# An attention and two mixture layers in one kernel: another order of the first loads, and the expert embeddings normalized in another stage

## The chip, the cores and the metric

The kernel runs on one core of one Trainium2 chip. The metric is the device time of one execution in microseconds (us). The kernel before takes 813.03 us, the median of three runs.

## The reference

Three layers follow each other, all in float32.

```python
attn = softmax(mask(q @ k.T / 8)) @ v          # 4 batches, 8 heads, 576 tokens, 64 wide
x = attn as [2304, 512]                        # heads side by side
x = ((x @ w_a) * (x @ w_b)) @ w_out            # w_a, w_b: 512 x 1536; w_out: 1536 x 512
en = expert_emb / (norm(expert_emb) + 1e-6)    # 8 x 512
logits = (x / (norm(x) + 1e-6)) @ en.T / tau   # the best of 8 experts for each token
out = gate * (relu(x @ w1[e]) @ w2[e])
```

The mask keeps a window of 32 keys in four heads, and every fourth of 128 keys in the other four. `w_a`, `w_b` and `w_out` are float64 in memory, so they come as 64-bit words ("doubles"), which the kernel turns into float32 itself.

## The kernel before, in words

The order of all instructions is written out by hand (`tc.manual_schedule()`, L1027): each engine, and each DMA queue, works through its own instructions in program order. SyncE (SP) issues nearly all loads and stores, one queue in program order; an issue that waits for a buffer holds all issues behind it.

**Precision.** Every large matrix product is made of three products of high and low parts (`mm3`, L582: high by high, high by low, low by high). `split` (L545) makes the parts: ScalarE (ACT) copies the high part (L546), VectorE (DVE) or GpSimd (POOL) subtracts it for the low part (L547).

**Doubles.** `conv_load(i)` (L495) loads block i of 18 (twelve of the a/b weights, 0 to 11, six of the output weights, 12 to 17; 1 MB each) into one of two `c64` buffers, or into the buffer of `wo` for blocks 2, 5, 8, 11. `conv_steps(i)` (L513) converts it in four steps: one on ACT (L526) and three on DVE (L528, L530, L532). `conv_store` (L508) stores the result for the later batches.

**First attention** (loop at L1047, blocks i = 0 to 12). In block i the scores of row block i are made (mask and `sc` on TensorE, PE, L410 and L416; `amx` on DVE, L426; `least` on POOL), the exponentials of block i-1 (ACT, L439), the transposes of block i-3 (L452) and the product with `v` of block i-4 (L468), whose result is split into `x0h` (ACT, L483) and `x0l` (DVE, L485). Between them stand one warm-up matmul (`keep_warm`, L762), steps of the conversion of doubles 0 and 1 as `CONV_STEPS` says, four quarter splits of `ab` 0 as `SPLIT0` says (`ab_split_part`, L549), and the first a/b products in blocks 10 and 11. The scores of block i use the banks of block i-2, so they wait for its exponentials. `qkt` and `vt` each have two buffers and come in thirds of a batch, three blocks each.

**Steps f = 0 to 11 of a batch** (`f_step`, L605). Each makes one 128-wide column block of x @ w_a and x @ w_b in four PSUM banks (`mm`), multiplies them (`g`, L619), and carries one block of the next batch's attention along. At f the split of `ab` f+1 is made; in batch 0 the doubles of block f+2 are converted, and block f+5 is loaded (L636). In batch 0 the exponentials of the attention follow the split on ACT.

**x1(b)** (`x1_run`, L707) makes the output projection of batch b in twelve steps; each needs a split of `wo`, made one step ahead (`x1_weights`, L680). In x1(0) the conversion of doubles 14 to 17 goes along, two steps for each block: the ACT step stands ahead of the split in even steps.

**Embeddings.** `setup` (f=2) loads them into `esb`, a tile of the `cv` pool beside the `c64` buffers. `setup2` (L140) normalizes them on DVE with a Newton iteration (`inv_norm`, L114), in the middle of f=6 of batch 0. `setup_en` (L148), in f=10, stores them to memory, transposes them on PE and copies them. `open_rows` (L753) closes `cv` in step 10 of x1(0) and opens the pool of `rows` and `en_a` in its place. At the start of batch 1 `en_a` and `en_b` are loaded (L1107), then `xs` is prefilled over the first four steps (L169), two issues ahead of each `ab_load` (L540).

The constants that the change touches stand at L50 to L57.

Of the kernel before, what the change touches and what calls it, by code (L numbers as in the profile page):

```python
# [48 lines left out]
N_WARM = 1  # L49
CONV_STEPS = (0, 0, 0, 0, 1, 1, 1, 1, 0, 1, 1, 1, 1)  # L50
CONV1 = 3
SPLIT0 = (8, 8, 9, 9)
PRE = (10, 11)
TEVAC_DVE = 5
ORDER = (0, 1, 1, 2, 3, 2)
LAG = 3
WARM_TO = 10  # L57
REBIAS = 2.0 ** -112
# [22 lines left out]
def fused_kernel(ctx: ExitStack, tc: tile.TileContext, qk, v, wab, wout, w1, w2, emb, tau, cst, msk, out, dbg=None):  # L81
# [31 lines left out]

    def inv_norm(ss, p, n, extra=None):  # L114
        x = ss
        yi = rt.tile([128, 8], I32, tag="nyi", name="nyi")[:p, :n]
        y = rt.tile([128, 8], F32, tag="ny", name="ny")[:p, :n]
        t = rt.tile([128, 8], F32, tag="nt", name="nt")[:p, :n]
        nc.vector.tensor_scalar(out=yi, in0=x.bitcast(I32), scalar1=1, scalar2=None, op0=ALU.logical_shift_right)
        nc.vector.tensor_scalar(out=y.bitcast(I32), in0=yi, scalar1=-1.0, scalar2=float(0x5F3759DF), op0=ALU.mult, op1=ALU.add)  # L120
        for _ in range(3):
            nc.vector.tensor_tensor(out=t, in0=y, in1=x, op=ALU.mult)
            nc.vector.tensor_tensor(out=t, in0=t, in1=y, op=ALU.mult)
            nc.vector.tensor_scalar(out=t, in0=t, scalar1=-0.5, scalar2=1.5, op0=ALU.mult, op1=ALU.add)
            nc.vector.tensor_tensor(out=y, in0=y, in1=t, op=ALU.mult)
        nc.vector.tensor_tensor(out=t, in0=y, in1=x, op=ALU.mult)
        nc.vector.tensor_scalar(out=t, in0=t, scalar1=1e-6, scalar2=None, op0=ALU.add)
        if extra is not None:
            nc.vector.tensor_tensor(out=t, in0=t, in1=extra, op=ALU.mult)
        nc.vector.reciprocal(out=y, in_=t)  # L130
        return y

# [7 lines left out]
    def setup2(e_sb, t_sb):  # L140
        junk = rt.tile([128, DM], BF16, tag="jl", name="ejunk", bufs=1)[:E, :]
        ss = rt.tile([E, 1], F32, tag="ess", name="ess", bufs=1)
        nc.vector.scalar_tensor_tensor(out=junk, in0=e_sb, scalar=1.0, in1=e_sb, op0=ALU.mult, op1=ALU.mult, accum_out=ss)
        rinv = inv_norm(ss, E, 1, extra=t_sb)
        nc.vector.tensor_scalar(out=e_sb, in0=e_sb, scalar1=rinv, scalar2=None, op0=ALU.mult)
        return e_sb

    def setup_en(junk):  # L148
        nc.sync.dma_start(out=en_d, in_=junk)
        tp = ps.tile([128, 4, E], F32, tag="rps", name="etp")  # L150
# [344 lines left out]
    def conv_load(i):  # L495
        if i < len(conv_src):
            if i < NF and i % 3 == 2:
                c64[i] = mp.tile([128, 2048], I32, tag="wo", name="c64w", bufs=1)
            else:
                c64[i] = cv.tile([128, 2048], I32, tag="c64", name="c64")  # L500
# [44 lines left out]
    def split(raw, hi, lo, eng=None):  # L545
        nc.scalar.activation(out=hi, in_=raw, func=AF.Copy)  # L546
        (eng or nc.vector).tensor_tensor(out=lo, in0=raw, in1=hi.bitcast(F32), op=ALU.subtract)  # L547

    def ab_split_part(n, q):  # L549
        if q == 0:  # L550
            ab_hl[n] = (ap.tile([128, 1024], F32R, tag="abh", name="abh"), ap.tile([128, 1024], F32R, tag="abl", name="abl"))
        w = slice(256 * q, 256 * q + 256)
# [4 lines left out]
    def ab_split(n):  # L557
        if n < n_ab:
            hl = (ap.tile([128, 1024], F32R, tag="abh", name="abh"), ap.tile([128, 1024], F32R, tag="abl", name="abl"))
            split(ab_raw.pop(n), *hl)  # L560
# [44 lines left out]
    def f_step(b, f, at_cur, at_mid, at_prev, extra, extra2):  # L605
# [27 lines left out]
        if f < NF - 2:  # L633
            ab_load(n + 2)
        if b == 0 and n != 9:
            conv_load(n + 5 if n < 9 else n + 4)  # L636
        cg = iter(())
# [42 lines left out]
    def x1_weights(b, i, n_i):  # L680
# [3 lines left out]
        if b == 0:  # L684
            conv_store()
            if i % 2 == 0:
                x1_conv[:] = [conv_steps(NF + 2 + i // 2)]
# [7 lines left out]
        if b == 0:  # L695
            conv(x1_conv[0], 1)
            if i % 2:
                conv_load(NF + 4 + i // 2)
        if not last:
# [6 lines left out]

    def x1_run(b, rows_at, hook):  # L707

# [3 lines left out]
        for i in range(NF):  # L712
            x1_weights(b, i, NF)
            if i == 0:
                g_lows()
            if i == rows_at:
                open_rows()
            hook(i)
# [308 lines left out]
    with tc.manual_schedule():  # L1027
# [19 lines left out]
        for i in range(NJ + LAG + 1):  # L1047
            if i in (3, 6, 9):
                load_qk()
            if i == CONV1:  # L1050
                conv_load(1)
                nc.sync.dma_start(out=c_sb, in_=cst)
            if i in (5, 9):
                load_v()
            if i == 6:
# [8 lines left out]
            if LAG + 1 <= i:  # L1064
                gr[i - LAG - 1].av()
            keep_warm(N_WARM if i < WARM_TO else 0, "mm1" if (i + 1 - LAG) % 2 else "tp")
            if 1 <= i < NJ + 1:
# [18 lines left out]
        for b in range(B):  # L1086
# [9 lines left out]
            for f in range(NF):  # L1096
# [15 lines left out]
                if b == 0 and f == 2:  # L1112
                    es.append(setup())
                if b == 0 and f == 6:
                    extra2.append(lambda: es.append(setup2(*es[0])))
                if b == 0 and f == 10:
                    extra2.append(lambda: setup_en(es[1]))
                if b == 1 and f < 4:
# [8 lines left out]
            if not last:  # L1127
                x1_run(b, 10 if b == 0 else None, lambda i: [next(steps, None) for _ in range(2)])
                for _ in steps:
# [228 lines left out]
```

## Time and profile before

| | |
|---|---|
| runs | 812.54, 813.03, 814.74 us (median 813.03) |
| profiled execution | 813.63 us, span 811.80 us |
| PE busy | 789.0 us, 97% |
| weight loads of PE busy | 729.0 us, 90% |
| DVE busy | 519.7 us, 64% |
| ACT busy | 410.5 us, 51% |
| POOL busy | 217.4 us, 27% |
| mean granted clock of TensorE | 0.987 of full speed |
| moved by DMA | 136.18 MB, mean 168 GB/s |

The span is what the profiler sees of one execution; the time of that execution has some 1.8 us around it. A row of a timeline has a start and a duration in us, the engine, the line of the kernel, the operation, output and inputs, and how often it stands there in a row; in square brackets is the idle time of its engine just before it and what ended it. Matmuls overlap, so they start closer together than their durations say. A granted clock of 1.00 is 2.4 GHz, one of 0.50 is 1.2 GHz.

### The profile page before, as it was taken

How to read it: one execution, taken by the hardware profiler on the slowest of the kernel's cores; microseconds unless marked ns; L12 is line 12 of the kernel's file. 1: busy time of each engine (PE TensorE's matmuls, PEld its weight loads, DVE VectorE, ACT ScalarE, POOL GpSimd, SP SyncE). 2: the span in 40 equal slices, each digit the busy share in tenths (PEclk: the TensorE clock that was granted, in tenths of full speed). 3: DMA queues.
4: the chain of work that ended last, by engine and by line, in shares of the span. 5: the costliest groups of instructions: out<-in, count | busy, mean ns of one | idle time of the engine just before them, and what ended most of it. 6: DMA issues, size and time to landing. Idle time of an engine off the chain costs nothing.

```text
span 811.8 us, 15994 instructions
## 1 busy us (share of the span) xinstructions
PE 789.0 (97%) x6112; PEld 729.0 (90%) x6112; DVE 519.7 (64%) x1153; ACT 410.5 (51%) x1014; POOL 217.4 (27%) x274
## 2 busy tenths in 40 slices
PE   7999998999999999999999999999999999999995
PEld 4799887789999889999989999999898999999994
DVE  4788888738876426787745884455666565666670
ACT  5666565345654225565324443454564544755651
POOL 3343244016353303544221334331110001111111
PEclk9899999999999999999999999999999999999998
DMA  9886676799433322241153222635565636655720
GB/s 288 297 253 205 222 217 230 251 322 342 156 105 108 125 78 80 94 134 61 51 165 117 92 78 91 222 130 197 183 208 191 203 125 194 209 166 183 234 77 26
DMA packets 40295, 136.18 MB, mean 168 GB/s; under 512 B 4084, under 2 KB 4340, under 8 KB 37777
## 3 DMA queue, kind: packets, MB, share of 16 engines
q1 hardware_dynamic: 37120, 125.54, 47.4%
q0 software_dynamic: 3088, 9.52, 3.1%
q8 instruction: 50, 0.82, 0.4%
q14 instruction: 37, 0.30, 0.1%
HBM read 109.67 MB, written 25.80 MB: 167 GB/s over the span
## 4 chain that ended last, share of the span: by engine, by line
PE 77%; issue 6%; DVE 6%; DMA 5%; ACT 5%; POOL 0%; POOLq 0%; DVEq 0%; SPq 0%
PE mm L584 11%; PE mm L586 10%; PE mm L585 10%; PE xr L585 4%; PE xr L586 4%; PE xr L584 4%; PE hp L585 3%; PE hp L586 3%; PE hp L584 3%; PE ytp L586 2%; PE ytp L585 2%; PE ytp L584 2%; DMA out_dram<-yo,ixi 2%; PE av L468 2%; PE sc L416 2%
## 5 line engine op out<-in xcount | busy, mean ns | idle before, releaser
L584 PE MATMUL mm<-x0h,abh 128*128 128x288 f32 x768 | 235.0, 306 | 1.5 <-DVE g L619 1.5
L586 PE MATMUL mm<-x0h,abl 128*128 128x288 f32 x768 | 226.8, 295 | 0.0
L585 PE MATMUL mm<-x0l,abh 128*128 128x288 f32 x768 | 226.7, 295 | 0.0
L584 PEld LDWEIGHTS mm<-x0h,abh 128*128 128x128 f32 x768 | 144.6, 188 | 6.7 <-DVE g L619 1.6
L585 PEld LDWEIGHTS mm<-x0l,abh 128*128 128x128 f32 x768 | 144.8, 188 | 0.0
L586 PEld LDWEIGHTS mm<-x0h,abl 128*128 128x128 f32 x768 | 144.6, 188 | 0.0
L623 POOL TENSOR_TENSOR gl<-g,gh 128x288 fp32r<-128x288 f32 x96 | 94.6, 991 | 114.7 <-ACT gh L622 114.6
L547 DVE TENSOR_TENSOR wl<-raw,wh 128x1024 fp32r<-128x1024 f32 x60 | 73.0, 1222 | 53.1 <-ACT wh L546 52.9
L547 DVE TENSOR_TENSOR wo<-wor,wo 128x512 fp32r<-128x512 f32 x60 | 46.4, 774 | 66.2 <-ACT wo L546 61.6
L982 POOL DMA_INDIRECT out_dram<-yo,ixi x23 | 27.3, 1188 | 204.6 <-ACT yo L981 157.9
L619 DVE TENSOR_TENSOR g<-a,mm 128x288 f32<-128x288 f32 x96 | 43.3, 451 | 54.9 <-PE mm L586 47.2
L546 ACT ACTIVATE wo<-wor 128x512 fp32r<-128x512 f32 x60 | 37.8, 630 | 78.6 <-PE xr L586 54.3
L622 ACT ACTIVATE gh<-g 128x288 fp32r<-128x288 f32 x96 | 42.4, 442 | 66.2 <-DVE g L619 66.2
L584 PE MATMUL hp<-xTh,wh 128*128 128x352 f32 (+6 forms) x224 | 68.9, 308 | 0.0
L546 ACT ACTIVATE abh<-abr 128x1024 fp32r<-128x1024 f32 (+1 forms) x51 | 51.1, 1007 | 33.2 <-DVE abr L532 20.8
L585 PE MATMUL hp<-xTl,wh 128*128 128x352 f32 (+6 forms) x224 | 67.7, 302 | 0.0
L586 PE MATMUL hp<-xTh,wl 128*128 128x352 f32 (+6 forms) x224 | 67.6, 302 | 0.0
L547 DVE TENSOR_TENSOR abl<-abr,abh 128x1024 fp32r<-128x1024 f32 x47 | 57.4, 1221 | 15.8 <-ACT abh L546 15.0
L546 ACT ACTIVATE wh<-raw 128x1024 fp32r<-128x1024 f32 x64 | 67.0, 1053 | 0.0
L434 POOL TENSOR_SCALAR least<-amx 128x4 f32<-128x4 f32 x36 | 23.5, 652 | 152.3 <-DVE amx L431 100.2
L584 PE MATMUL xr<-wo,gh 128*128 128x512 f32 x156 | 61.8, 396 | 2.4 <-ACT wo L546 2.1
L585 PE MATMUL xr<-wo,gh 128*128 128x512 f32 x156 | 61.8, 396 | 0.6 <-DVE wo L547 0.6
(218 smaller groups left out, 1715.6 us busy)
## 6 DMA issues: line engine op xcount, KB each, us to landing
raw<-in_w_dram SPq DMA_DIRECT2D x64, 512.0 KB, 4.2
abr<-wab SPq DMA_DIRECT2D x36, 512.0 KB, 3.4
wor<-wout SPq DMA_DIRECT2D x24, 512.0 KB, 3.4
qkt<-in_qk_dram SPq DMA_DIRECT2D x12, 832.0 KB, 8.4
c<-in_wab_dram SPq DMA_DIRECT2D x8, 1024.0 KB, 12.7
vt<-in_v_dram SPq DMA_DIRECT2D x12, 576.0 KB, 4.6
xs<-rows SPq DMA_DIRECT2D x8, 781.5 KB, 16.6
wab<-abr SPq DMA_DIRECT2D x12, 512.0 KB, 5.0
```

What stands on the lines that cost most here:

```text
L416: nc.tensor.matmul(out=self.sc[odd][64 * q:64 * q + 64, h, :], lhsT=t[64 * p:64 * p + 64, pr, 64 * jj:64 * jj + 64], rhs=t[64 * p:64 * p + ...
L434: nc.gpsimd.tensor_scalar(out=self.least, in0=mx, scalar1=0.125, scalar2=None, op0=ALU.mult)
L468: nc.tensor.matmul(out=self.o[64 * p:64 * p + 64, pr, :], lhsT=t[:, jj, 64 * h:64 * h + 64], rhs=self.aT[:, pr, 64 * (p ^ pr % 2):64 * (p ...
L546: nc.scalar.activation(out=hi, in_=raw, func=AF.Copy)
L547: (eng or nc.vector).tensor_tensor(out=lo, in0=raw, in1=hi.bitcast(F32), op=ALU.subtract)
L584: nc.tensor.matmul(out=out_, lhsT=lh, rhs=rh, start=first, stop=False)
L585: nc.tensor.matmul(out=out_, lhsT=lh, rhs=rl, start=False, stop=False)
L586: nc.tensor.matmul(out=out_, lhsT=ll, rhs=rh, start=False, stop=last)
L619: nc.vector.tensor_tensor(out=g, in0=a, in1=acc[1, hf], op=ALU.mult)
L622: nc.scalar.activation(out=g_hl[0][:, f, t], in_=g, func=AF.Copy)
L623: nc.gpsimd.tensor_tensor(out=g_hl[1][:, f, t], in0=g, in1=g_hl[0][:, f, t].bitcast(F32), op=ALU.subtract)
L982: nc.gpsimd.indirect_dma_start(out=out, out_offset=bass.IndirectOffsetOnAxis(ap=self.ixi[e][:m, t:t + 1], axis=0), in_=yo[:m, :], in_offse ...
```

## The change

In the first attention the second `vt` leaves the list at the head of the kernel and is issued in block 4; the third comes in block 6. Double 1 and the constants are issued in block 5 instead of 3. The conversion of double 1 begins in block 11 instead of 9, and its last two steps come after the loop. The quarter splits move from blocks 8 and 9 to 7 and 8. The warm-up matmuls stand in blocks 0 to 3 and 9 to 11 instead of 0 to 9.

The high and the low part of an `ab` block lie in one tile with two buffers, where they were two tiles with two buffers each. Doubles 14 and 15 are loaded into such buffers instead of `c64`. Double 14 is issued in f=11 instead of f=10, 16 right behind it instead of in step 1 of x1(0); 15 and 17 are issued in step 0 of x1(0) instead of f=11 and step 3.

The normalization of the embeddings becomes a generator with five pieces, which run in steps 5 to 9 of x1(0) instead of f=6; its store is issued with the last piece instead of in f=10. Transposes and copies of the embeddings, and the opening of the pool of `rows`, move to step 11 of x1(0).

```diff
-CONV_STEPS = (0, 0, 0, 0, 1, 1, 1, 1, 0, 1, 1, 1, 1)
-CONV1 = 3
-SPLIT0 = (8, 8, 9, 9)
+CONV_STEPS = (0, 0, 0, 0, 1, 1, 1, 1, 0, 0, 0, 1, 1)
+CONV1 = 5
+SPLIT0 = (7, 7, 8, 8)
...
-ORDER = (0, 1, 1, 2, 3, 2)
+ORDER = (0, 1, 1, 2, 3)
-WARM_TO = 10
+WARM_TO = 12
...
-    def inv_norm(ss, p, n, extra=None):
+    def inv_norm_steps(ss, p, n, extra=None):
...
             nc.vector.tensor_tensor(out=y, in0=y, in1=t, op=ALU.mult)
+            yield y
...
         nc.vector.reciprocal(out=y, in_=t)
-        return y
+        yield y
+
+    def inv_norm(ss, p, n, extra=None):
+        return list(inv_norm_steps(ss, p, n, extra))[-1]
...
-        rinv = inv_norm(ss, E, 1, extra=t_sb)
+        for rinv in inv_norm_steps(ss, E, 1, extra=t_sb):
+            yield
         nc.vector.tensor_scalar(out=e_sb, in0=e_sb, scalar1=rinv, scalar2=None, op0=ALU.mult)
-        return e_sb
+        nc.sync.dma_start(out=en_d, in_=e_sb)
+        yield
 
     def setup_en(junk):
-        nc.sync.dma_start(out=en_d, in_=junk)
...
+            elif i in (NF + 2, NF + 3):
+                c64[i] = ap.tile([128, 2048], I32, tag="ab", name="c64a")
             else:
                 c64[i] = cv.tile([128, 2048], I32, tag="c64", name="c64")
...
+    def ab_tile():
+        t = ap.tile([128, 2, 1024], F32R, tag="ab", name="ab")
+        return t[:, 0, :], t[:, 1, :]
...
-            hl = (ap.tile([128, 1024], F32R, tag="abh", name="abh"), ap.tile([128, 1024], F32R, tag="abl", name="abl"))
+            hl = ab_tile()
...
-        if b == 0 and n != 9:
-            conv_load(n + 5 if n < 9 else n + 4)
+        if b == 0 and n < 9:
+            conv_load(n + 5)
+        if n == NF - 1:
+            conv_load(NF + 2)
+            conv_load(NF + 4)
...
         if b == 0:
             conv_store()
+            if i == 0:
+                conv_load(NF + 3)
+                conv_load(NF + 5)
...
-            if i % 2:
-                conv_load(NF + 4 + i // 2)
...
+            if i in (4, 6, 9):
+                load_v()
             if i == CONV1:
                 conv_load(1)
                 nc.sync.dma_start(out=c_sb, in_=cst)
-            if i in (5, 9):
-                load_v()
...
-            keep_warm(N_WARM if i < WARM_TO else 0, "mm1" if (i + 1 - LAG) % 2 else "tp")
+            keep_warm(N_WARM if i < 4 or NJ <= i < WARM_TO else 0, "mm1" if (i + 1 - LAG) % 2 else "tp")
...
-                if b == 0 and f == 6:
-                    extra2.append(lambda: es.append(setup2(*es[0])))
-                if b == 0 and f == 10:
-                    extra2.append(lambda: setup_en(es[1]))
+                if b == 0 and f == NF - 1:
+                    es.append(setup2(*es[0]))
...
-                x1_run(b, 10 if b == 0 else None, lambda i: [next(steps, None) for _ in range(2)])
+                def hook(i):
+                    for _ in range(2):
+                        next(steps, None)
+                    if b == 0 and 5 <= i < 11:
+                        next(es[1], None)
+                    if b == 0 and i == 11:
+                        setup_en(es[0][0])
+                        open_rows()
+
+                x1_run(b, hook)
```

## Rows read from the trace of the kernel before

**Rows 1.** The page, part 1: busy us, share of the span, instructions.

```profile
PE 789.0 (97%) x6112; PEld 729.0 (90%) x6112; DVE 519.7 (64%) x1153; ACT 410.5 (51%) x1014; POOL 217.4 (27%) x274
```

**Rows 2.** The timeline, blocks 5 to 8: start, us, engine, line, operation.

```profile
18.75 1.06 DVE L528 TENSOR_SCALAR abr<-c 128x1024 uint32<-128x1024 uint32 x1
...
19.64 0.92 PE L416 MATMUL sc<-qkt 64*64 64x96 f32 x16 [1.57 <-DMA qkt<-in_qk_dram]
...
25.00 0.61 DVE L426 TENSOR_REDUCE amx<-sc 128x2 f32<-128x192 f32 x2
...
26.57 0.33 PE L410 MATMUL sc<-mask_bf,id_bf 128*128 128x192 bf16 x2
...
26.80 0.33 ACT L439 ACTIVATE s<-sc,least 128x96 f32<-128x96 f32 x1
...
27.07 0.59 DVE L485 TENSOR_TENSOR x0l<-av,x0h 128x128 fp32r<-128x128 f32 x2 [0.57 <-ACT x0h L483]
...
27.57 1.22 DVE L532 SCALAR_TENSOR_TENSOR abr<-c,abr 128x1024 uint32<-128x1024 uint32 x1
```

**Rows 3.** Windows: stretch, busy us of five engines, PEclk, DMA share, GB/s.

```profile
20.00:21.00 1.00, 1.00 (x19) 0.75 (x12) 0.34 (x2) 0.00 (x0) 0.00 (x0) 0.50 0.78 306
...
140.00:145.00 5.00, 3.74 (x10) 2.75 (x11) 4.56 (x5) 1.74 (x4) 1.06 (x1) 0.74 1.00 322
...
165.00:170.00 5.00, 5.00 (x24) 4.14 (x23) 1.14 (x2) 1.74 (x3) 0.00 (x0) 1.00 1.00 332
```

**Rows 4.** The timeline, end of the first attention and f=0, as above.

```profile
35.13 0.69 DVE L528 TENSOR_SCALAR abr<-c 128x1024 uint32<-128x1024 uint32 x1
...
37.85 1.23 DVE L532 SCALAR_TENSOR_TENSOR abr<-c,abr 128x1024 uint32<-128x1024 uint32 x1
...
39.12 1.06 ACT L546 ACTIVATE abh<-abr 128x1024 fp32r<-128x1024 f32 x1 [1.10 <-DVE abr L532]
...
41.61 0.42 ACT L618 ACTIVATE a<-mm 128x288 f32<-128x288 f32 x1
...
42.00 0.34 PE L410 MATMUL sc<-mask_bf,id_bf 128*128 128x192 bf16 x2
```

**Rows 5.** The timeline, steps f=6 to f=8 of the first projection.

```profile
83.15 0.34 PE L410 MATMUL sc<-mask_bf,id_bf 128*128 128x192 bf16 x2
...
91.62 0.34 PE L410 MATMUL sc<-mask_bf,id_bf 128*128 128x192 bf16 x2
...
95.09 0.67 DVE L143 SCALAR_TENSOR_TENSOR ejunk<-esb 8x512 bf16<-8x512 f32 x1
...
97.79 0.69 PE L468 MATMUL av<-aT,vt 96*64 96x64 f32 x16
...
99.05 0.47 DVE L145 TENSOR_SCALAR esb<-esb,ny 8x512 f32<-8x512 f32 x1
...
103.13 0.57 PE L410 MATMUL sc<-mask_bf,id_bf 128*128 128x192 bf16 x2 [1.31 <-ACT s L439]
...
111.08 0.69 PE L468 MATMUL av<-aT,vt 96*64 96x64 f32 x16
```

**Rows 6.** The timeline, first four steps of x1(0).

```profile
139.24 1.14 ACT L526 ACTIVATE c<-c 128x1024 f32<-128x1024 f32 x1 [3.48 <-DMA c<-in_wout_dram]
...
146.98 1.11 ACT L526 ACTIVATE c<-c 128x1024 f32<-128x1024 f32 x1 [5.24 <-DMA c<-in_wout_dram]
...
148.69 0.47 PE L584 MATMUL xr<-wo,gh 128*128 128x512 f32 x1
```

**Rows 7.** The timeline, end of x1(0) and start of batch 1 (SPq: DMA issues).

```profile
165.26 0.37 SPq L1107 DMA_DIRECT2D en_a<-en_d  x1
...
171.41 0.39 PE L584 MATMUL xr<-wo,gh 128*128 128x512 f32 x1
...
182.03 1.06 ACT L546 ACTIVATE abh<-abr 128x1024 fp32r<-128x1024 f32 x1 [0.41 <-DMA abr<-wab]
...
189.18 0.29 PE L586 MATMUL mm<-x0h,abl 128*128 128x288 f32 x1
```

More of the change, by code (lines that the diff above doesn't have):

```diff
@@ L547, in split @@
         (eng or nc.vector).tensor_tensor(out=lo, in0=raw, in1=hi.bitcast(F32), op=ALU.subtract)
+    def ab_tile():
+        t = ap.tile([128, 2, 1024], F32R, tag="ab", name="ab")
+        return t[:, 0, :], t[:, 1, :]
     def ab_split_part(n, q):
         if q == 0:
-            ab_hl[n] = (ap.tile([128, 1024], F32R, tag="abh", name="abh"), ap.tile([128, 1024], F32R, tag="abl", name="abl"))
+            ab_hl[n] = ab_tile()
         w = slice(256 * q, 256 * q + 256)
@@ L705, in x1_weights, with x1_run @@
                 ab_split(NF * (b + 1))
-    def x1_run(b, rows_at, hook):
+    def x1_run(b, hook):
         c0 = CARRY * (1 - b % 2)
@@ L715, in x1_run @@
                 g_lows()
-            if i == rows_at:
-                open_rows()
             hook(i)
```

## The prediction

> **What bounds the kernel now.** I read the page first, for the share of each engine, then TensorE's waits in order of time, then the stretches around the change. TensorE (PE) is busy 97% of the span [rows 1], so only a place where PE waits, or runs at the lower clock, can give or take time. The change touches four such places: the first attention, the step f=6 of the first a/b projection, the first output projection x1(0), and the start of batch 1. Everything later is left as it is.
>
> The profiled execution took 813.63 us (811.80 of span, 1.83 around it), 0.60 above the median of the three runs, 813.03. The sum below is made against 813.63, and its difference is then put on the median.
>
> **A. First attention (blocks i).** PE waits 1.57 us for the third `qkt` and starts at 19.64 [rows 2]; a microsecond later its granted clock is 0.50, the 1.2 GHz level [rows 3]. The new order takes one `vt` (0.59 MB) from ahead of that `qkt`: at 0.322 MB per us (the rate of another full stretch [rows 3]) 1.8 us, so the wait is covered. That is the gain one sees. What is late next is VectorE (DVE). `SPLIT0` moves the first quarter splits from i=8 to i=7, the very block whose last DVE operation (L532) makes the data they read. ScalarE (ACT) keeps program order, so its half of the split waits for L532, and the exponentials of block 7 queue behind it. When does L532 end? L528 runs from 18.75 to 19.81, whatever `qkt` does. A block of DVE work takes, from 25.00 to the end of L532 at 28.79, 3.79 us, 0.57 of it a wait, so 3.22 [rows 2]. Two blocks behind 19.81 end at 26.25. Two quarters of a split (half of its 1.06 us [rows 4], with handovers 0.65) put the exponentials of block 7 at 26.9, against 26.80 now [rows 2]. So what PE gains is waited away on ACT, and I take the start of f=0 as unmoved; bounds -0.4, since ACT later has one operation less ahead of block 8, and +0.6.
>
> Then f=0. In the old order L528 and L530 of the second conversion stand between the last `x0l` pieces; in the new one they come behind the last of them. That is 0.69 and 1.22 us more [rows 2, 4] (L530 has the size of L532) ahead of L532, less at most 0.4 us by which that `x0l` can come sooner, since it waits for ACT: L532 ends 1.5 us later. Behind it wait the split of `ab` 1 (39.12) and the exponentials of the next attention, which end by 41.61; PE's scores of f=1 need the banks that these read and start at 42.00 [rows 4]. So 0.4 us of slack is used up first; 1.1 is left, with two handovers +1.3.
>
> Four or five warm-up matmuls fewer in blocks 4 to 8 cost nothing by themselves, but PE now idles in several pieces between about 24 and the late exponentials. Waits of 1.57 us and less went ahead of the fall in rows 3, so I expect the fall again, only later. One fall is priced by f=8 below: 0 to 1.8 us. Part of it lies beside ACT, so I take 1.2. **A = +2.5**, bounds -4.4 (rival 1) and +3.7.
>
> The Trainium skill, page "SBUF — State Buffer", section "SBUF: two separate sides", says that VectorE and GpSimd exclude each other on a shared port pair for a whole instruction. The trace leans that way: the same L528 took 1.06 us in block 5 and 0.69 in block 10 [rows 2, 4]. By this rule L530 and L532 of blocks 6 and 7 would each be held as L528 is, 0.37 us, and the sum would end 0.7 us higher; without it, as above.
>
> **B. f=6.** DVE spends 4.4 us, from 95.09 to 99.52, on 22 small instructions of the normalization [rows 5]. The g-multiply behind them frees a PSUM bank that PE needs, and the conversion behind that holds the split and ACT's exponentials. PE starts f=7 at 91.62 and f=8 at 103.13, 11.51 us, where the step before took 8.47 (from 83.15): 3.04 lost. In f=8 the clock is down: its `av` starts 7.95 us into the step against 6.17 in f=7, another 1.78 [rows 5]. Without the chain 4.82 comes back. Bounds: -3.0 (if the clock falls anyway) and -4.8; no row speaks for the former. **B = -4.8.** The instructions go to steps 5 to 9 of x1(0) in five pieces, the first (with the square, 0.67, and a round) some 1.8 us. They cost nothing there while DVE has room: it is busy 1.14 of 5 us at 165 to 170 [rows 3]. Without that cover the first piece would cost up to 1. The four transposes of the embeddings cost PE the same in either place.
>
> **C. The doubles in x1(0).** ACT starts on double 14 at 139.24, after waiting 3.48 us for its DMA, and on 15 at 146.98, after 5.24; the split behind 15 lets PE start its fourth step at 148.69 [rows 6]. 14 is issued at the end of f=10 now. In the new order it stands at the start of f=11, behind the store of 12 (0.52 MB) and a `vt` (0.59 MB), which follow it now. The buffer of `ab` 10 is free earlier, but SyncE (SP) keeps its order and the store waits for the same conversion as 14 does now; so 14 can't go earlier. 1.11 MB more ahead at 0.322 per us [rows 3] is 3.5 us. 15 is issued behind the store of 13, as now, but has 16 ahead of it: 1.05 MB, 3.3 us, and 4.9 with that store counted too, which today is partly moved by then; I take 3.6. ACT keeps its order, so the split for the fourth step moves with it and PE with the split: **C = +3.6**, bounds 0 (15 lands no later) and +4.9. 16 and 17 land earlier, which gives nothing, since PE doesn't wait for them today.
>
> **D. Start of batch 1.** `en_a` lies in the rows pool, where the c64 buffers and the embeddings (`esb`) lay. Its load is issued at 165.26 today, with the transposes of `esb` long past. In the new order these stand ahead of PE's twelfth step, which starts at 171.41 [rows 7], so the load goes out near 171.8, 6.5 us later. Behind it on SP: `en_b`, two prefills of `xs`, and the load of `abr` 14. The queue is full here (332 GB/s [rows 3]), and ACT already waits 0.41 us for that `abr` before it takes it at 182.03 [rows 7]. 6.5 later is 188.5; the split's 1.06 on ACT and 1.23 on DVE (as long as L532) end near 190.8. The first matmul of f=2 that reads the low half starts at 189.18 today [rows 7]: 1.6, with the handover 1.7 us of wait. **D = +1.7**, bounds 0 (`en_a` doesn't wait for the transposes) and +3.5 (with a fall of the clock, 1.8).
>
> The a/b halves in one tile cost nothing: each half is still written and read by its own slices, and its buffer is free a full step before; else a handover of 0.1 us in each of 48 steps.
>
> **Sum:** 2.5 - 4.8 + 3.6 + 1.7 = +3.0. The profiled execution would be 816.6, the median **816.0**.
>
> **Rivals.** (1) *The first attention keeps its gain.* Besides the wait of 1.57, PE needed 6.93 us from 19.64 to 26.57 [rows 2] at the lower clock, some 4.1 at the full one (half, and the handovers): 4.4 together. If the conversion is done by 24 instead of 26.25, ACT isn't held, A is -4.4 and the sum -3.9: 809.1, faster. For it: PE and DMA allow it. Against it: DVE's rows leave no gap. (2) *The doubles land in time*, because four loads in flight move more than 0.322 per us: C is 0, the sum -0.6, 812.4. For it: ACT's waits were partly for loads not yet issued; against it: the DMA share is 1.00 there [rows 3]. (3) *The clock holds* in the first attention: A +1.3, the sum +1.8, 814.8. (4) *It falls twice*: D +3.5, and the first attention at its +0.6: +5.4, 818.4. That the change doesn't do what it says holds for double 14 alone, which goes out later than now; that is in C.
>
> **How the numbers follow.** Forecast 0.35 and rival (4) 0.10: slower by over 0.3%, 0.45. 0.3% is 2.4 us, about what a measurement of this kernel can tell from no change. Rivals (2) 0.22 and (3) 0.13: within 0.3%, 0.35. Rival (1): faster, 0.20. The range runs from 809.0 to 818.8: it leaves out rival (1) with C at 0 as well, and the far ends of A, C and D together. The slower cases alone span 815.5 to 818.8.
>
> **What would show it.** Right: no PE wait for `qkt` near 18; ACT waiting for L532 before the quarter splits near 26; f=8 starting 8.5 us after f=7; ACT waiting over 6 us for double 14; `en_a` issued only when PE is in its twelfth step, and ACT waiting some 6 us for `abr` 14. Wrong: exponentials of block 7 before 25 us (A); a wait for double 15 no longer than today's 5.24 with PE's fourth step no later behind its first (C); no PE wait in the first three steps of batch 1 (D).

## The result, and the profile after

| | kernel before | changed kernel |
|---|---|---|
| median of the timed runs, us | 812.54 (7 runs, 810.47 to 814.74) | 817.02 (7 runs, 815.18 to 818.58) |
| ratio of the times | 1 | 1.0053, 95% interval 1.0036 to 1.0070 |
| profiled execution, us (span) | 813.63 (811.8) | 815.76 (814.0) |

The change costs some 4.3 us (2.9 to 5.7 by the interval): slower, as forecast, at 817.0 where 816.0 was predicted. The two profiled executions lie only 2.1 us apart: that of before is 1.1 above its median, that of the change 1.3 below its own. Stages are therefore read from the traces, totals from the medians.

TensorE is as busy as before: 788.0 us, 97% of the span, where [rows 1] have 789.0.

**First attention.** The timeline of the changed kernel (start, us, engine, line, operation, idle before and what ended it). The lines of the program have moved: L410, L416, L439, L447, L452, L457, L468, L530, L532, L546 and L547 of before are L415, L421, L444, L452, L457, L462, L473, L537, L539, L553 and L554 here.

```profile
17.12 0.56 PE L421 MATMUL sc<-qkt 64*64 64x96 f32 x16
...
20.53 0.83 POOL L452 TENSOR_TENSOR s<-s,asm 128x384 f32<-128x384 f32 x1 [0.68 <-DVE asm L451]
...
20.81 1.63 DVE L537 SCALAR_TENSOR_TENSOR abr<-c,abr 128x1024 uint32<-128x1024 uint32 x1
...
23.62 0.69 PE L473 MATMUL av<-aT,vt 96*64 96x64 f32 x16 [0.97 <-DVE aT L462]
...
24.67 1.26 DVE L539 SCALAR_TENSOR_TENSOR abr<-c,abr 128x1024 uint32<-128x1024 uint32 x1
...
24.90 0.79 PE L457 MATMUL atp<-ident,s 128*96 128x128 f32 x4 [0.60 <-POOL s L452]
...
25.96 0.72 ACT L553 ACTIVATE ab<-abr 128x256 fp32r<-128x256 f32 x2 [4.21 <-DVE abr L539]
...
26.59 0.32 ACT L444 ACTIVATE s<-sc,least 128x96 f32<-128x96 f32 x1
...
28.50 1.12 PE L473 MATMUL av<-aT,vt 96*64 96x64 f32 x16 [2.81 <-ACT aT L464]
...
37.98 0.34 PE L415 MATMUL sc<-mask_bf,id_bf 128*128 128x192 bf16 x2
...
44.78 0.57 PE L415 MATMUL sc<-mask_bf,id_bf 128*128 128x192 bf16 x2 [1.00 <-DVE ab L554]
...
52.23 0.34 PE L415 MATMUL sc<-mask_bf,id_bf 128*128 128x192 bf16 x2
```

The wait of 1.57 us for `qkt` [rows 2] is gone. In its place ACT stands idle for 4.21 us until L539 has made what the quarter splits read, and everything behind them in ACT's program waits too: the exponentials of block 7, then the copy `aT`, for which PE waits 2.81 us. f=0 starts at 37.98 (36.36 before), f=1 at 44.78 (42.00, [rows 4]). Windows of the changed kernel (stretch, its length, busy us of PE, PEld, DVE, ACT and POOL, PEclk, DMA share, GB/s):

```profile
20.00:26.00 6.00, 3.84 (x60) 2.44 (x58) 5.60 (x16) 1.78 (x11) 1.87 (x3) 0.94 1.04 304
26.00:35.00 9.00, 6.36 (x48) 4.93 (x48) 3.05 (x14) 6.64 (x31) 4.61 (x7) 0.50 0.90 310
```

and the same two of the kernel before:

```profile
20.00:26.00 6.00, 6.00 (x73) 4.09 (x67) 4.25 (x12) 1.80 (x11) 1.27 (x3) 0.50 0.57 158
26.00:35.00 9.00, 8.03 (x117) 5.84 (x116) 4.88 (x19) 8.54 (x36) 5.46 (x8) 0.98 1.03 367
```

The clock's fall isn't avoided, it only comes later: PE waits in pieces, ahead of the fall for DVE's `aT` (0.97 us) and GpSimd's `s` (0.60), is granted 0.50 (1.2 GHz) from about 25.3 us, and stays at that level to about 35.5, where the kernel before was back at full speed from 26.3. The splits in block 7 don't bring on the fall itself: in old_split (below), where they stand in block 8, the clock falls at 25.3 us too, but is back at 32.1.

**f=6 to f=8.** The timeline of the changed kernel:

```profile
94.63 0.34 PE L415 MATMUL sc<-mask_bf,id_bf 128*128 128x192 bf16 x2
...
100.80 0.69 PE L473 MATMUL av<-aT,vt 96*64 96x64 f32 x16
...
103.11 0.34 PE L415 MATMUL sc<-mask_bf,id_bf 128*128 128x192 bf16 x2
...
109.27 0.69 PE L473 MATMUL av<-aT,vt 96*64 96x64 f32 x16
```

f=8 starts 8.48 us behind f=7 (11.51 before). From `av` to `av` of the two steps it is 8.47 us where [rows 5] have 13.29 (97.79 to 111.08): 4.82 given back.

**x1(0).** The timeline of its first four steps in the changed kernel (L533 and L595 are L526 and L584 of before). The row at 133.27 is the first matmul of PE's first step:

```profile
133.27 0.50 PE L595 MATMUL xr<-wo,gh 128*128 128x512 f32 x1
...
140.45 1.10 ACT L533 ACTIVATE c64a<-c64a 128x1024 f32<-128x1024 f32 x1 [5.92 <-DMA c64a<-in_wout_dram]
...
142.13 0.80 PE L595 MATMUL xr<-wo,gh 128*128 128x512 f32 x1 [4.47 <-ACT wo L553]
...
146.69 1.16 ACT L533 ACTIVATE c64a<-c64a 128x1024 f32<-128x1024 f32 x1 [3.76 <-DMA c64a<-in_wout_dram]
...
148.70 0.69 DVE L554 TENSOR_TENSOR wo<-wor,wo 128x512 fp32r<-128x512 f32 x1
...
150.72 0.39 PE L595 MATMUL xr<-wo,gh 128*128 128x512 f32 x1
```

The first matmul of PE's first step in the kernel before:

```profile
135.33 0.39 PE L584 MATMUL xr<-wo,gh 128*128 128x512 f32 x1
```

Windows of the changed kernel, and under them of the kernel before:

```profile
142.00:148.00 6.00, 5.86 (x13) 4.29 (x14) 4.66 (x6) 2.08 (x4) 4.47 (x5) 0.50 1.01 424
138.00:148.00 10.00, 5.86 (x13) 4.29 (x14) 5.07 (x6) 3.63 (x5) 4.47 (x5) 0.67 1.01 421
```

```profile
142.00:148.00 6.00, 6.00 (x20) 4.75 (x20) 3.27 (x3) 1.02 (x2) 0.36 (x1) 0.72 0.94 313
138.00:148.00 10.00, 7.61 (x24) 5.58 (x25) 5.86 (x6) 3.53 (x6) 1.06 (x1) 0.83 0.98 325
```

ACT waits 5.92 us for double 14 (3.48, [rows 6]) and PE 4.47 us in its second step (2.07 before). ACT takes double 15 at 146.69, where [rows 6] have 146.98; but x1(0) began 2.06 us sooner, so counted from PE's first step 15 comes 1.8 us later (13.4 against 11.65). It holds nothing all the same: the split that stands behind it in ACT's program is done at 149.39, and PE's fourth step starts at 150.72 without waiting. That step starts 17.45 us behind the first (13.36 before), because of the long wait at the head of the second step and of the clock, which is at 0.50 throughout that step, to 148 us.

**Start of batch 1.** The timeline of the changed kernel (SPq: DMA issues):

```profile
173.03 0.32 SPq L1120 DMA_DIRECT2D en_a<-en_d  x1
...
188.81 1.06 ACT L553 ACTIVATE ab<-abr 128x1024 fp32r<-128x1024 f32 x1 [5.50 <-DMA abr<-wab]
...
190.00 0.56 PE L421 MATMUL sc<-qkt 64*64 64x96 f32 x16
...
191.18 0.40 PE L597 MATMUL mm<-x0h,ab 128*128 128x288 f32 x1
...
198.78 0.56 PE L421 MATMUL sc<-qkt 64*64 64x96 f32 x16
```

`en_a` is issued 7.8 us later than in [rows 7] and ACT waits 5.50 us for `abr` 14, but PE feels little of it: f=3 starts 8.78 us behind f=2, against 8.29 before. Beyond that point the two traces run at one distance to the end.

### The profile page after: what moved, and what is told of

It reads as the page before. It is cut to its first block, busy times and chain, and to the rows that moved or that the text cites. A ratio compares the mean times of both kernels' runs of the same rounds, so it can differ in the third digit from the quotient of the medians.

```text
span 814.0 us, 15992 instructions
## 1 busy us (share of the span) xinstructions
PE 788.0 (97%) x6109; PEld 728.6 (90%) x6109; DVE 521.4 (64%) x1153; ACT 409.8 (50%) x1014; POOL 219.1 (27%) x274
## 4 chain that ended last, share of the span: by engine, by line
PE 68%; issue 10%; DMA 9%; DVE 6%; ACT 5%; POOL 0%; SPq 0%; POOLq 0%; DVEq 0%; ACTq 0%
PE mm L595 10%; PE mm L597 9%; PE mm L596 9%; DMA out_dram<-yo,ixi 6%; PE xr L595 4%; PE xr L596 4%; PE xr L597 4%; PE hp L595 2%; PE hp L596 2%; PE hp L597 2%; ACT s L444 2%; PE av L473 2%; DMA abr<-wab 2%; DVE abr L539 2%; DVE abr L535 1%
## 5 line engine op out<-in xcount | busy, mean ns | idle before, releaser
L595 PE MATMUL mm<-x0h,ab 128*128 128x288 f32 x768 | 235.1, 306 | 0.1
L597 PE MATMUL mm<-x0h,ab 128*128 128x288 f32 x768 | 226.7, 295 | 0.1
L596 PE MATMUL mm<-x0l,ab 128*128 128x288 f32 x768 | 226.7, 295 | 0.0
L595 PEld LDWEIGHTS mm<-x0h,ab 128*128 128x128 f32 x768 | 144.5, 188 | 5.5 <-PE wp L779 0.4
L597 PEld LDWEIGHTS mm<-x0h,ab 128*128 128x128 f32 x768 | 144.5, 188 | 0.4 <-DVE ab L554 0.3
L596 PEld LDWEIGHTS mm<-x0l,ab 128*128 128x128 f32 x768 | 144.7, 188 | 0.1
L634 POOL TENSOR_TENSOR gl<-g,gh 128x288 fp32r<-128x288 f32 x96 | 98.2, 1029 | 117.0 <-ACT gh L633 116.9
L554 DVE TENSOR_TENSOR wl<-raw,wh 128x1024 fp32r<-128x1024 f32 x60 | 73.0, 1222 | 53.3 <-ACT wh L553 53.2
L554 DVE TENSOR_TENSOR wo<-wor,wo 128x512 fp32r<-128x512 f32 x60 | 46.5, 775 | 65.7 <-ACT wo L553 61.1
L553 ACT ACTIVATE wo<-wor 128x512 fp32r<-128x512 f32 x60 | 37.8, 630 | 84.3 <-PE xr L597 60.1
L553 ACT ACTIVATE ab<-abr 128x1024 fp32r<-128x1024 f32 (+1 forms) x51 | 51.1, 1006 | 47.2 <-DVE abr L539 25.0
L554 DVE TENSOR_TENSOR ab<-abr,ab 128x1024 fp32r<-128x1024 f32 x47 | 57.5, 1223 | 22.0 <-ACT ab L553 21.3
L595 PE MATMUL hp<-xTh,wh 128*128 128x352 f32 (+6 forms) x224 | 68.9, 308 | 0.0
L595 PE MATMUL xr<-wo,gh 128*128 128x512 f32 x156 | 62.6, 401 | 5.6 <-ACT wo L553 4.5
L553 ACT ACTIVATE wh<-raw 128x1024 fp32r<-128x1024 f32 x64 | 67.1, 1054 | 0.0
L597 PE MATMUL xr<-wo,gl 128*128 128x512 f32 x156 | 61.7, 396 | 0.0
```

Of the source, the lines that this page charges most:

```text
L595: nc.tensor.matmul(out=out_, lhsT=lh, rhs=rh, start=first, stop=False)
L596: nc.tensor.matmul(out=out_, lhsT=lh, rhs=rl, start=False, stop=False)
L597: nc.tensor.matmul(out=out_, lhsT=ll, rhs=rh, start=False, stop=last)
L634: nc.gpsimd.tensor_tensor(out=g_hl[1][:, f, t], in0=g, in1=g_hl[0][:, f, t].bitcast(F32), op=ALU.subtract)
```

## The experiments

Eleven kernels. Each row of the table is read from one profiled execution: the start of f=0; f=1 behind f=0; f=8 behind f=7; the length of x1(0), from ACT's last copy of a projection bank to the first copy of x1's rows; f=3 of batch 1 behind its f=2. The ratio is to runs of the kernel before made beside it (medians 812.4 to 813.1), with its 95% interval; kernels that were not timed together are best compared by their ratios.

| kernel | f=0 | f=1 | f=8 | x1(0) | f=3 | median us | ratio |
|---|---|---|---|---|---|---|---|
| before | 36.36 | 5.64 | 11.51 | 36.93 | 8.29 | | 1 |
| changed | 37.98 | 6.80 | 8.48 | 39.79 | 8.78 | 817.02 | 1.0053 (1.0036 to 1.0070) |
| first_only | 38.73 | 6.80 | 11.72 | 38.20 | 8.29 | 817.99 | 1.0055 (1.0038 to 1.0072) |
| norm_only | 37.34 | 5.64 | 8.49 | 37.38 | 8.75 | 810.32 | 0.9959 (0.9944 to 0.9973) |
| doubles_only | 36.48 | 5.64 | 11.47 | 38.54 | 8.28 | 814.77 | 1.0021 (1.0010 to 1.0032) |
| old_split | 35.34 | 6.79 | 8.49 | 39.49 | 8.49 | 813.11 | 0.9997 (0.9984 to 1.0010) |
| old_warm | 38.14 | 6.81 | 8.49 | 38.63 | 8.81 | 815.70 | 1.0031 (1.0019 to 1.0044) |
| split_warm | 34.98 | 6.81 | 8.49 | 40.03 | 8.84 | 812.00 | 0.9983 (0.9963 to 1.0002) |
| early14 | 35.45 | 6.80 | 8.47 | 36.58 | 8.87 | 810.16 | 0.9971 (0.9952 to 0.9991) |
| norm_loads | 38.45 | 5.64 | 8.49 | 37.14 | 8.90 | 811.38 | 0.9968 (0.9951 to 0.9985) |
| split_steps | 36.49 | 5.65 | 8.49 | 39.09 | 8.48 | 811.09 | 0.9986 (0.9976 to 0.9997) |
| first_before | 35.32 | 5.65 | 8.48 | 37.81 | 8.29 | 808.61 | 0.9954 (0.9940 to 0.9969) |
| first_mended | 35.52 | 6.80 | 8.49 | 38.26 | 8.29 | 810.29 | 0.9973 (0.9959 to 0.9986) |

### The three parts, each alone in the kernel before

**first_only**: the constants and loads of the first attention.

```
-CONV_STEPS = (0, 0, 0, 0, 1, 1, 1, 1, 0, 1, 1, 1, 1)
-CONV1 = 3
-SPLIT0 = (8, 8, 9, 9)
-ORDER = (0, 1, 1, 2, 3, 2)
-WARM_TO = 10
+CONV_STEPS = (0, 0, 0, 0, 1, 1, 1, 1, 0, 0, 0, 1, 1)
+CONV1 = 5
+SPLIT0 = (7, 7, 8, 8)
+ORDER = (0, 1, 1, 2, 3)
+WARM_TO = 12
-            if i in (5, 9):
+            if i in (4, 6, 9):
                 load_v()
-            keep_warm(N_WARM if i < WARM_TO else 0, "mm1" if (i + 1 - LAG) % 2 else "tp")
+            keep_warm(N_WARM if i < 4 or NJ <= i < WARM_TO else 0, "mm1" if (i + 1 - LAG) % 2 else "tp")
```

> The kernel before with the new order of the first attention alone (order of loads, conversion steps, quarter splits, warm-up matmuls). Theory, step A with the size that the two traces give: the scores of f=0 start near 38.0 us instead of 36.4, those of f=1 near 44.8 instead of 42.0, and the time is 3 us above the kernel before (the forecast had 2.5). Rival: the loss of 3 us seen there in the changed kernel comes from the a/b halves that share one buffer; then the first attention alone gives 0 or a gain of up to 4.4.

Measured: 0.55% slower, 4.5 us (3.1 to 5.9) where 3 was expected; f=0 at 38.73, f=1 at 45.53. The loss of the change has its seat here, and the shared a/b buffer, which this kernel doesn't have, no part in it.

**norm_only**: the normalization out of f=6, with the hook of x1(0) as in the change.

```
-                if b == 0 and f == 6:
-                    extra2.append(lambda: es.append(setup2(*es[0])))
-                if b == 0 and f == 10:
-                    extra2.append(lambda: setup_en(es[1]))
+                if b == 0 and f == NF - 1:
+                    es.append(setup2(*es[0]))
```

> The kernel before with the move of the embeddings alone: normalization in steps 5 to 9 of x1(0), the transposes and the opening of the rows pool in step 11. Theory, steps B and D: f=8 starts 8.5 us behind f=7 and the clock stays up in f=8, which gives 4.8; the late load of the normalized embeddings gives back 0.5 to 1.7 at the start of batch 1; together 3.1 to 4.3 us below the kernel before. Rival: the work on VectorE only moves, and x1(0) waits for it; then within 1 us of the kernel before.

Measured: 0.41% faster, 3.3 us (2.2 to 4.6). The timeline of this kernel, `av` of f=7 and of f=8:

```profile
98.77 0.69 PE L473 MATMUL av<-aT,vt 96*64 96x64 f32 x16
...
107.24 0.69 PE L473 MATMUL av<-aT,vt 96*64 96x64 f32 x16
```

8.47 us from `av` to `av` again, 4.82 less than before: B holds. x1(0) takes 37.38 us, between the 36.93 and 38.20 of two kernels without the normalization in it, so its new place hides it. f=3 of batch 1 is 0.46 later: D, alone.

**doubles_only**: the a/b halves in one buffer and the loads of doubles 14 to 17.

```
+            elif i in (NF + 2, NF + 3):
+                c64[i] = ap.tile([128, 2048], I32, tag="ab", name="c64a")
...
-        if b == 0 and n != 9:
-            conv_load(n + 5 if n < 9 else n + 4)
+        if b == 0 and n < 9:
+            conv_load(n + 5)
+        if n == NF - 1:
+            conv_load(NF + 2)
+            conv_load(NF + 4)
...
+            if i == 0:
+                conv_load(NF + 3)
+                conv_load(NF + 5)
...
-            if i % 2:
-                conv_load(NF + 4 + i // 2)
```

> The kernel before with the new loads of doubles 14 to 17 alone (the a/b halves in one buffer, two loads at the start of f=11 and two at that of x1(0)). Theory, step C: ScalarE waits some 2.4 us longer for double 14, the first matmul of x1's second step starts later, and the time is 2.8 to 3.6 us above the kernel before. Rival: what x1(0) loses in the changed kernel is caused by the normalization that was put into it; then the doubles alone give 0 within 0.5.

Measured: 0.21% slower, 1.7 us (0.8 to 2.6), between theory and rival. The timeline of this kernel:

```profile
141.66 1.10 ACT L528 ACTIVATE c64a<-c64a 128x1024 f32<-128x1024 f32 x1 [5.84 <-DMA c64a<-in_wout_dram]
...
143.34 0.80 PE L590 MATMUL xr<-wo,gh 128*128 128x512 f32 x1 [4.39 <-ACT wo L548]
```

These are the waits of the changed kernel without its normalization: the doubles cause them. The three parts add to +0.35% (0.55 - 0.41 + 0.21), just under the interval of the change (0.36 to 0.70); since each part has an uncertainty of 0.1 to 0.2%, the sum and the change can't be told apart.

### Inside the first attention

**old_split**, in the changed kernel: `SPLIT0 = (8, 8, 9, 9)` again.

```
-SPLIT0 = (7, 7, 8, 8)
+SPLIT0 = (8, 8, 9, 9)
```

> The changed kernel with the quarter splits of the first a/b weights back in blocks 8, 8, 9, 9. Theory: the splits in block 7 make ScalarE wait for the last conversion operation (4.2 us), and the exponentials of block 7 queue behind that; without them these exponentials start near 25 us instead of 26.6, f=0 starts 1 to 1.6 us sooner than in the changed kernel, and the time is 1 to 1.6 us below it. Rival: TensorE at half clock, with the late end of the second conversion, sets f=1 whatever ScalarE does in block 7; then within 0.4 us of the changed kernel.

Measured: 813.11, 3.9 us below the changed kernel (4.5 by the ratios); the intervals of the two ratios lie apart. The timeline of this kernel:

```profile
23.78 0.34 ACT L444 ACTIVATE s<-sc,least 128x96 f32<-128x96 f32 x1 [1.63 <-POOL least L439]
...
26.32 1.12 PE L473 MATMUL av<-aT,vt 96*64 96x64 f32 x16
...
26.36 0.72 ACT L553 ACTIVATE ab<-abr 128x256 fp32r<-128x256 f32 x2 [0.26 <-DVE abr L539]
...
35.34 0.34 PE L415 MATMUL sc<-mask_bf,id_bf 128*128 128x192 bf16 x2
```

The exponentials of block 7 run at 23.78 instead of 26.59, `av` has no wait, and the splits themselves come only 0.4 us later, since L539 sets them in either place. Its window of the same stretch:

```profile
26.00:35.00 9.00, 8.72 (x81) 6.44 (x81) 3.83 (x17) 6.66 (x24) 4.58 (x7) 0.66 1.01 340
```

PE is busy 8.72 of 9 us instead of 6.36 and is back at full speed at 32.1 us instead of 35.5. Theory right, its size (1 to 1.6) too small: f=0 starts 2.64 us sooner. It counted ACT's delay and not the longer stretch at half clock that goes with it; no run separates the two.

**old_warm**, in the changed kernel: the warm-up matmuls of before.

```
-WARM_TO = 12
+WARM_TO = 10
-            keep_warm(N_WARM if i < 4 or NJ <= i < WARM_TO else 0, "mm1" if (i + 1 - LAG) % 2 else "tp")
+            keep_warm(N_WARM if i < WARM_TO else 0, "mm1" if (i + 1 - LAG) % 2 else "tp")
```

> The changed kernel with one warm-up matmul in each of blocks 4 to 8 and none from block 10 on, as before. Theory, from step A: these matmuls cost nothing, and the clock falls near 25.6 us as in the changed kernel, because TensorE still waits for ScalarE in blocks 6 to 8; the time is within 0.5 us of the changed kernel's. Rival: they fill the idle pieces and hold the granted clock at 1.00 through blocks 7 to 11; then f=0 starts some 2 us sooner and the time is 1 to 3 us below the changed kernel's.

f=0 at 38.14 and the clock down all the same. Its window:

```profile
26.00:35.00 9.00, 5.90 (x47) 4.65 (x47) 3.59 (x15) 6.69 (x31) 4.62 (x7) 0.52 0.94 308
```

The median, 815.70, is 1.3 below the changed kernel's (1.8 by the ratios), with overlapping intervals. That is more than the 0.5 of the theory and the size of the rival, but the rival's mechanism isn't there: the clock doesn't hold and no stage of the first attention gains. In the profiled execution the difference (1.35) lies almost wholly in x1(0), 38.63 instead of 39.79, which the edit doesn't touch. The theory stands by the rows; by the time it isn't shown.

**split_warm**: both edits.

> The changed kernel with the quarter splits back in blocks 8, 8, 9, 9 and with the old warm-up matmuls too. Beside the run with the old splits alone (813.1, with the clock at 0.50 from 25.6 to 32 us). Theory: the fall comes all the same, and the time is within 0.5 us of 813.1. Rival: without ScalarE's wait the warm-up matmuls are enough to hold the clock; f=0 starts near 33.5 us instead of 35.3, and the time is 1 to 2 us below 813.1.

f=0 at 34.98, 0.36 before old_split; 812.00, 1.1 below it, with overlapping intervals. Its window:

```profile
26.00:35.00 9.00, 7.33 (x86) 5.88 (x87) 3.88 (x17) 6.73 (x25) 4.60 (x7) 0.81 1.00 340
```

Here the matmuls do go with a later and shorter stretch at the lower level (from 29.5 to 32.8 us; 0.81 in the mean where old_split has 0.66), and f=0 hardly starts sooner: at the higher clock PE waits for others instead (1.32 us for GpSimd's `s` ahead of the transposes at 28.23). By f=0 that is nearer the theory, though not for its reason, since the fall did come later; the time is in the rival's range (1 to 2). The run doesn't decide between them.

**split_steps**: old_split with the second conversion back in blocks 9 to 12 as well.

```
-CONV_STEPS = (0, 0, 0, 0, 1, 1, 1, 1, 0, 0, 0, 1, 1)
+CONV_STEPS = (0, 0, 0, 0, 1, 1, 1, 1, 0, 1, 1, 1, 1)
```

> The changed kernel with the old quarter splits and with the second conversion back in blocks 9 to 12. Beside the old quarter splits alone (813.1; f=0 starts at 35.34 us and f=1 6.79 behind it, where the kernel before has 5.64). Theory, the second part of step A: the two conversion operations that stand behind the last x0l pieces delay the last one, and the split of ab 1 and the exponentials wait for it; without them f=1 starts 5.6 to 5.8 us behind f=0, and the time is 0.7 to 1.1 us below 813.1. Rival: VectorE has no gap for them in blocks 9 to 12 either, f=0 starts as much later; then within 0.4 us of 813.1.

The timeline of this kernel:

```profile
36.49 0.34 PE L415 MATMUL sc<-mask_bf,id_bf 128*128 128x192 bf16 x2
...
42.14 0.34 PE L415 MATMUL sc<-mask_bf,id_bf 128*128 128x192 bf16 x2
```

f=1 comes 5.65 us behind f=0, as in every kernel with the old steps (6.79 to 6.81 in every kernel with the new ones). But f=0 starts 1.15 later than in old_split, so f=1 starts at 42.14 here and 42.13 there: the rival, by the rows of one execution each. The other traces agree: without splits in block 7, f=1 starts at 41.8 to 42.3 with the new steps (four executions) and at 41.0 to 44.1 with the old ones (six). So by the rows the two conversion operations cost as much ahead of f=0 as behind it. The time doesn't settle it: the median is 2.0 lower, 0.9 by the ratios, which is the theory's size, with overlapping intervals.

**norm_loads**, in the kernel before: norm_only with the new order of loads alone.

```
-ORDER = (0, 1, 1, 2, 3, 2)
+ORDER = (0, 1, 1, 2, 3)
-            if i in (5, 9):
+            if i in (4, 6, 9):
                 load_v()
```

> The kernel before with the move of the embeddings and with the new order of the loads (qkt ahead of the second vt), and with the old conversion steps, quarter splits, warm-up matmuls and loads of doubles. Beside the move of the embeddings alone (810.3). Theory: the wait for the third qkt goes, DVE's conversion of the first a/b weights ends some 1.5 us sooner or at the same time, and with the old splits ScalarE is not held; 0 to 1.6 us below 810.3. Rival: the clock falls once in the first attention anyway and later than before, when TensorE is bound by itself; then 0 to 1.5 us above 810.3.

811.38 against the 810.32 of norm_only (0.7 by the ratios), f=0 at 38.45 against 37.34: on the rival's side, though the intervals overlap. The wait for `qkt` is gone here too. A window of this kernel:

```profile
23.00:36.00 13.00, 12.55 (x107) 8.99 (x107) 6.59 (x23) 8.27 (x34) 5.75 (x9) 0.50 0.90 277
```

PE is busy 12.55 of 13 us, and at half clock all the time. That is where the gain of the loads went in this execution.

### The doubles, and what beats both kernels

**early14**: old_split with double 14 issued first at the start of f=11.

```
+        if n == NF - 1:
+            conv_load(NF + 2)
         if b == 0:
             conv_store()
...
         if n == NF - 1:
-            conv_load(NF + 2)
             conv_load(NF + 4)
```

> The changed kernel with the old quarter splits and with the load of double 14 issued at the start of f=11 ahead of the store of 12 and the load of vt, instead of behind them. Theory, step C: the 1.11 MB ahead of it cost 14 some 2.4 to 3.5 us; ScalarE waits that much less for it, x1(0) starts its second step 2 us or more sooner, and the time is 1.5 to 2.8 us below the 813.1 of the old quarter splits alone. Rival: the loads share the queue's rate whatever their order (four in flight), or x1's loss comes from the clock's fall and not from the wait; then within 0.5 us of 813.1.

Measured: 810.16, 2.9 below old_split (2.1 by the ratios, whose intervals overlap by a hair), where 1.5 to 2.8 was expected. SP's issues in the changed kernel:

```profile
131.95 0.33 SPq L518 DMA_DIRECT2D wout<-wor  x1
132.77 0.34 SPq L389 DMA_DIRECT2D vt<-in_v_dram  x1
133.29 0.34 SPq L508 DMA_DIRECT2D c64a<-in_wout_dram  x1
```

and in this one, with ACT's two conversions and PE's second step:

```profile
124.64 0.33 SPq L508 DMA_DIRECT2D c64a<-in_wout_dram  x1
129.47 0.33 SPq L518 DMA_DIRECT2D wout<-wor  x1
...
131.97 1.12 ACT L533 ACTIVATE c64a<-c64a 128x1024 f32<-128x1024 f32 x1
...
137.25 0.50 PE L596 MATMUL xr<-wo,gh 128*128 128x512 f32 x1 [1.84 <-DVE wo L554]
...
142.33 1.14 ACT L533 ACTIVATE c64a<-c64a 128x1024 f32<-128x1024 f32 x1 [6.29 <-DMA c64a<-in_wout_dram]
```

The load's own buffer was free 4.8 us before the store ahead of it could go (124.64 and 129.47). Put first, it lands before ACT asks for it, PE waits 1.84 us in its second step instead of 4.53 (old_split), and x1(0) takes 36.58 us instead of 39.49. In the three kernels that issue 14 first (this one and the next two) PE's fourth step starts 13.4 to 14.6 us behind its first, in the six with the late 14 it is 16.2 to 17.7, in the four with the old loads 13.0 to 14.9. So C is double 14's place on SP.

**first_before** (first attention as before; embeddings; doubles as in early14; the hook, that is the calls placed in each step of x1(0), two steps sooner for the normalization, and the rows pool in step 10) and **first_mended** (the same with the first attention of split_warm).

```
-                    if b == 0 and 5 <= i < 11:
+                    if b == 0 and 3 <= i < 9:
                         next(es[1], None)
-                    if b == 0 and i == 11:
+                    if b == 0 and i == 10:
                         setup_en(es[0][0])
                         open_rows()
```

> The first attention as before; the move of the embeddings, with the normalization two steps of x1(0) sooner and the transposes and the rows pool in step 10 instead of 11; the new loads of doubles, with double 14 issued ahead of the store of 12. Theory, steps B, C and D: B gives its 4.8 us, C costs nothing, and the load of the normalized embeddings goes out some 5 us sooner, so that f=3 of batch 1 starts 8.3 us behind f=2 (8.8 in the changed kernel); the time is 4 to 5 us below the kernel before, under both kernels. Rival: what B gives is lost in x1(0) to the clock; then 2 to 3 us below the kernel before, as with the embeddings alone (810.3).

> The same as the run before it, but with the first attention as changed save for the quarter splits and the warm-up matmuls, which are as before (f=0 at 34.98 us in the run with these two). Theory: the sums of the stages add; the first attention is 0.3 us later than that of the kernel before at the splits of f=0, and the time is within 0.7 us of the run with the first attention as before. Rival: the new order of loads gives its 1.57 us once ScalarE isn't held; then 1 to 2 us below that run.

first_before: 808.61, 3.7 us below the kernel before (2.5 to 4.9), just short of the 4 to 5 expected, and under both kernels; from norm_only it can't be told. D is gone in it, f=3 following f=2 by 8.29 us, and x1(0) took 37.81. first_mended: 1.7 above it (1.5 by the ratios, with overlapping intervals), where within 0.7, or a gain, was expected; neither shows. By the rows it starts f=0 0.2 and f=1 1.35 later, but first_before's start of f=0 is the earliest of the four executions with the old first attention. Without the splits in block 7 the new first attention is no better than the old one, as far as these runs tell.

## Why the prediction was right, and where its steps were not

**The direction and the size** were right: +3.0 forecast, +4.3 measured (2.9 to 5.7). The signs of all four terms held; three of their sizes are off. That the sum came so near is in part luck: A was put too low, C and D too high, and the errors cancel.

**A, +2.5.** The mechanism was right: `qkt` no longer waits, DVE is late next, ACT waits for its last operation before the quarter splits (L539 ended at 25.93, forecast 26.25), the exponentials of block 7 come at 26.59 (forecast 26.9), the clock falls again. The step that failed is "I take the start of f=0 as unmoved". The exponentials of block 7 are as early as before, but in the kernel before PE's slow stretch was then over, and here it had just begun: PE at 0.50 works through blocks 8 to 11 and f=0 starts 1.6 us later. Over all executions f=0 starts at 37.98 to 38.73 with the splits in block 7 (three) and at 34.98 to 35.52 without (four, same steps): 3.0 us, which is all of A at f=1. The "+1.3" for the second conversion has its size (1.15), but by the rows it isn't a loss: split_steps shows the same 1.15 gained at f=0, though its time leaves 0.9 us open. So A's pieces were 0, 1.3 and 1.2, where the rows show 3.0 for the splits with the longer stretch at half clock and nothing for the rest. By the rows A is 3.0 (f=2 at 52.23, 49.23 before); first_only's times say 4.5 (3.1 to 5.9).

L537 took 1.63 us beside a GpSimd multiply (POOL L452 at 20.53), where its like of before, L530, took 1.22; L539 took 1.26 beside the end of another. The Trainium skill, page "SBUF — State Buffer", section "SBUF: two separate sides", has a VectorE operation with two SBUF inputs and a GpSimd operation that reads SBUF exclude each other on a shared port pair for the whole instruction: of the two holds of 0.37 us that the forecast put beside the sum by this rule, the first shows (0.41), the second does not (0.04).

**B, -4.8.** Right to the digit in the rows (4.82 in the pair, 4.82 in norm_only). Its cover held. (The trace has 21 instructions in the chain, not 22.)

**C, +3.6.** The sum named the wrong double. PE's fourth step did come 4.1 us later behind its first (17.45 against 13.36), but 15, which was to land 3.6 us late and hold that step, didn't hold it: it came 1.8 us later behind PE's first step, and the split behind it was done 1.3 us before PE's step. The queue moved 421 GB/s from 138 to 148 us where the forecast took 322. That is rival (2)'s reason, and it came true; its result did not. The step that failed is that 14's longer wait (3.48 to 5.92 us), which the forecast saw, was charged nothing of its own: it puts PE's second step 3.25 us later behind the first (8.86 against 5.61), and that step then runs at 0.50 throughout. That step doesn't use 14 at all: its split reads double 12, and 14 is in its way only because its conversion stands ahead of the split in ACT's program, as in A. (Putting that split first was not tried.) Nor did the split behind 15 hold PE up by much in the kernel before, as the forecast read [rows 6]: the third step took 2.72 us there, as undisturbed steps do, and only 0.31 us of wait lies in the fourth. In the profiled pair x1(0) lost 2.9 us. Over all executions it takes 38.5 to 40.0 us with the late double 14 (six, mean 39.3), 36.9 to 38.2 with the old loads (four, mean 37.4) and 36.6 to 38.3 with 14 issued first (three): a loss of 1.9, and doubles_only's times say 1.7. The forecast's remark that 14 "can't go earlier" holds only behind the store; early14 put it ahead.

**D, +1.7.** The chain was right (`en_a` out in PE's twelfth step, ACT waiting 5.50 us for `abr` 14, forecast some 6), the size was not: 0.5. The forecast set the new end of the split, 190.8, against PE's place in the old kernel, 189.18. The split did end at 191.13, but PE itself stood 1.7 us later there (f=2 at 190.00, 188.31 before), through A, B and C. A wait has to be reckoned between two times of the same kernel. In first_before, where the load of `en_a` goes out a step sooner, the loss is gone.

**The signs listed.** Four of six came as written; ACT's wait for 14 was 5.92 instead of over 6, and its wait for `abr` 14 was 5.50 instead of some 6. Of the three marks of a wrong prediction one half came: the wait for 15 was 3.76, under 5.24, while PE's fourth step was still later behind its first.

**What stays open.** The stages of the profiled pair add to +2.1 and the parts' times to +2.9, against +4.3; the intervals allow it, and no row shows where the rest lies. How much of A is ACT's hold and how much the longer stretch at half clock was not separated. Why the queue moved 421 instead of 325 GB/s was not tried.

## What to carry to other kernels

When a wait is taken out at the head of a chain, follow the consumer that keeps program order: an operation put into the very block that makes its data holds everything behind it on that engine. A load that stands behind a waiting store on an in-order queue is late by the store's wait, so put the one that lands on the path first, and charge a delay to the first consumer that PE waits for. Small serial chains on VectorE are worth moving to a stage where that engine has room: that is the one part of the change that gained here (norm_only, 3.3 us).

## What the runs showed that was not expected

The same first attention, instruction for instruction, started f=0 at 36.36, 37.34, 36.48 and 35.32 us in the four executions that have it (before, norm_only, doubles_only, first_before): a stage's gain of one microsecond there can't be read from one trace.

The DMA share says little of the rate: 0.98 at 325 GB/s and 1.01 at 421, in the same 10 us of the two kernels.
